# Where a weight's double words are turned into floats: two integer steps on VectorE and two passes on ScalarE, in place of three and one

## The chip, the cores and the metric

The kernel runs on one core of a Trainium2 chip. Time is device time in microseconds (us), the median of the runs shown; a profiled execution has its own time and its own span, which is the time from its first to its last instruction. The engines are named as in the profile: PE is TensorE's matmul, PEld its weight load, DVE is VectorE, ACT is ScalarE, POOL is GpSimd, SP is SyncE, which here only issues DMAs.

## The reference, cut to what matters

Three layers follow each other on a batch of 4, 576 positions, 8 heads of 64, so a model width of 512.

1. Attention. q and k are rotated by position (rope), scores are scaled by 1/8, the row maximum is subtracted, exp, division by the sum plus 1e-9, product with v.
2. First block: `xn = (x - mean) / sqrt(var + 1e-6) * g_ln`, then `x + relu(xn @ w_ch1) @ w_ch2`, with w_ch1 of 512 x 2048 and w_ch2 of 2048 x 512.
3. Second block: `h = gelu(x @ w_in)`, split in u and v; v is normalised, mixed over positions by w_sg, given b_sg, multiplied by u; `x + gated @ w_out`.

The weights w_ch1, w_ch2, w_in and w_out arrive as 64-bit floats, and the kernel sees each as two 32-bit words: a low word L and a high word H. It makes 32-bit floats of them itself. The high word has the sign, the exponent and the first 20 bits of the fraction; three more bits of fraction are the top three of the low word. So a 32-bit float is the sign of H, the rest of H (its exponent moved to the 32-bit bias) shifted left by 3, and `L >> 29` in the three places that the shift leaves free.

## The kernel before, in words

**Attention** runs in 64 units: two heads of a pair, two halves of 288 queries (HQ), four pairs, four batch entries. A unit (`unit`) computes scores of 576 keys in five chunks of 128 (`scores`, L311) into the five PSUM banks of S, takes their maximum on DVE (mx, L334), then over partitions on POOL (am, L337). Either PE adds the negative maximum to S (`add`, L392) and ACT takes exp from PSUM (L395), or DVE subtracts it (`subtract`, L376) and ACT takes exp from SBUF (L381); the second way is used once all 32 weights of the first block are stored (`stored[0] == 32`). PV (L350) multiplies by v; ACT copies the result (L357) and the row of sums (L360). There is one S and one bank for PV, so the scores of the next unit can start only when exp has read this one's.

**The first block** (`up`, `down`, L655 to L657 and L685 to L687) needs, of a batch entry, its LN (`ln`, `rest`): L477 and L479 take the reciprocals of the sums, L492 spreads them by a matmul over the PV bank, L494 multiplies, L508 and L512 subtract the mean, L524 and L528 make the two halves xh and xl of the normalised input. Weights are used as a high and a low part (`w[:, 0]`, `w[:, 1]`), since a matmul reads a shortened form of a 32-bit float (the kernel's type fp32r); so each product is three matmuls.

**Conversion.** 32 weight tiles of 128 x 512 doubles belong to the first block, 12 more (8 of w_in, 4 of w_out) to the second. `double_parts` (L37 to L56) makes a tile's floats in parts, one instruction each: the DMA of 512 KB into cd (L44), an ACT pass that scales H by 2 to the power -112, read as a float, into ce (L48), and three DVE steps: shift left by 3 (L50), join the sign from H (L52), join `L >> 29` (L55). Then the caller casts to the high part on ACT (L635, L890) and subtracts it on DVE for the low part (L637, L892). The cd words have a stride of two words in these reads. Callers are `convert` for the 32 tiles and `Weights2.split` for the 12. There are four cd and two ce buffers (two and two for the 12), and of the 32, eleven weight buffers (tags w and wx); a later tile waits with its cast until PE has used up an earlier one. The loader (L611) reads stored weights again for the later batch entries, and starts when the last of the 32 tiles has got its buffer.

**Order.** `Sched` is a planner that runs while the kernel is built: every task yields an engine, an earliest time and an assumed duration, and the planner issues next the one that can start first; a task of better rank displaces it if it could start within 0.4 (HOLD) of the displaced one's duration. Ranks: attention 0, the ends of matmul groups 1, LN 2, loads about 3, conversion 4, the matmuls of the first block 5. Each engine then runs its instructions strictly in the planned order, so the assumed durations (0.68 us for an ACT pass, 0.45 for L50, 0.7 for L52 and for L55) settle the order, and the chip settles the times. The second block, from its second part on, is written in plain program order.

Of the kernel before, what the change touches and what calls it, by code (L numbers as in the profile page):

```python
# [9 lines left out]
AF = mybir.ActivationFunctionType  # L10
ALU = mybir.AluOpType
# [17 lines left out]
I32 = mybir.dt.int32  # L29
U32 = mybir.dt.uint32  # L30


def f32(ap):
    return ap.bitcast(F32)


def double_parts(nc, q, pool, src, bufs):  # L37

    n = src.shape[1]
    d = pool.tile([128, n, 2], I32, tag="cd", name="cd", bufs=bufs[0])
    q.dma_start(out=d.rearrange("p n t -> p (n t)"), in_=src.bitcast(I32))  # L44
    yield None
    H, L = d[:, :, 1], d[:, :, 0].bitcast(U32)
    e = pool.tile([128, n], I32, tag="ce", name="ce", bufs=bufs[1])
    nc.scalar.activation(f32(e), f32(H), AF.Copy, scale=2.0 ** -112)  # L48
    yield None
    nc.vector.tensor_scalar(e, e, 3, None, ALU.logical_shift_left)  # L50
    yield None
    nc.vector.scalar_tensor_tensor(e, H, -0x80000000, e, op0=ALU.bitwise_and, op1=ALU.bitwise_or)  # L52
    yield None
    u = e.bitcast(U32)
    nc.vector.scalar_tensor_tensor(u, L, 29, u, op0=ALU.logical_shift_right, op1=ALU.bitwise_or)  # L55
    yield f32(e)  # L56


# [66 lines left out]
def latest(*xs):  # L125

    return None if any(x is None for x in xs) else max(xs)


class Attn:  # L130
# [66 lines left out]
    def split(self, x, X, at):  # L197
        nc = self.nc
        e = yield "ACT", at + 0.1, 0.43
        nc.scalar.copy(X[:, 1, :], x)  # L200
        e = yield "DVE", e + 0.1, 0.47
        nc.vector.tensor_tensor(X[:, 0, :], x, f32(X[:, 1, :]), ALU.subtract)
        return e
# [220 lines left out]
def fused_kernel(ctx, tc, q, k, v, cs, cst, w12, wi, wo, wsg, wsg4, gb, out):  # L424
    nc = tc.nc
# [169 lines left out]
    def widx(key):  # L595
        return key[2] if key[1] == 0 else 16 + 4 * key[2] + key[3]

    def wtag():
        return "wx" if len(ring) < 32 and len(ring) % (WB + WX) >= WB else "w"

    def new_w(key):

        tag = wtag()
        ring[key] = tag, wb[tag].take()
        wt[key] = (M if tag == "w" else cpool).tile([128, 2, 512], F32R, tag=tag, name=tag, bufs=WB if tag == "w" else WX)
        return wt[key]
# [7 lines left out]
    def convert(n):  # L614
        key = wq[n]
        i = widx(key)
        e = yield "SP", lambda: latest(cdb.free(), 14.0), 0.6
        slot = cdb.take()
        parts = double_parts(nc, nc.sync, cpool, w12[i], (CB, 2))
        next(parts)  # L620
        if n < 31:
            C.task(convert(n + 1), 4)
        e = yield "ACT", lambda: latest(e + L_CONV, ceb.free()), 0.68
        ce = ceb.take()
        next(parts)
        yield "DVE", e + 0.1, 0.45
        next(parts)
        yield "DVE", 0.0, 0.7
        next(parts)
        e = yield "DVE", 0.0, 0.7  # L630
        s = next(parts)
        cdb.give(slot, e)
        e = yield "ACT", lambda: latest(e + 0.1, wb[wtag()].free()) if len(ring) == n else None, 0.63
        t = new_w(key)
        nc.scalar.copy(t[:, 0, :], s)  # L635
        e = yield "DVE", e + 0.1, 0.7
        nc.vector.tensor_tensor(t[:, 1, :], s, f32(t[:, 0, :]), ALU.subtract)  # L637
        ceb.give(ce, e)
        wat[key] = e + 0.1
        yield "SP", e + 0.1, 0.6  # L640
        nc.sync.dma_start(out=f32(wsc[i]), in_=f32(t))
        stored[0] += 1
# [76 lines left out]
    def mlp_pass(g, F, halves=(0, 1), ups=None):  # L719

        n = FG[g]
        seq = [(f, hh) for f in ups or range(n) for hh in halves]
        if F in (0, 16 // n - 1):
            seq.sort(key=lambda x: x[1])
        for f, hh in seq:
            yield 0, g, F, f, hh
        for c in range(4) if ups is None else ():
            for hh in halves:
                yield 1, g, F, c, hh

    def group0():
        yield from mlp_pass(0, 0, [0])
        yield from mlp_pass(0, 1, [0], range(AHEAD))
        yield from mlp_pass(0, 0, [1])
        yield from mlp_pass(0, 1, [1], range(AHEAD))
        yield from (x for x in mlp_pass(0, 1) if x[0] or x[3] >= AHEAD)
        for F in (2, 3):
            yield from mlp_pass(0, F)
# [64 lines left out]
    C.task(select(), 3.9)  # L803
    C.task(norms(), 2, lambda: over.append("norms"))
    C.task(convert(0), 4)
    C.task(loader(), 3.5)
    pctx = ExitStack()
    parts = [*group0(), *(x for g in range(1, NG) for F in range(16 // FG[g]) for x in mlp_pass(g, F))]
# [32 lines left out]
class Weights2:  # L841
# [22 lines left out]
    def split(self, i):  # L864
        nc, t, pool, cdb, ceb, stb = self.nc, self.t, self.pool, self.cdb, self.ceb, self.stb
        src, n, k, a, z = self.items[i]
        single = src.dtype == F32
        e = yield "SP", lambda: (stb if single else cdb).free() if n + "h" in t else None, 0.6
        slot = (stb if single else cdb).take()
        if single:  # L870
            s = pool.tile([128, 576], F32, tag="st", name="st")[:, 0:z - a]
            nc.sync.dma_start(out=s, in_=src)
            if k == 0:
                nc.sync.dma_start(out=t["b"], in_=self.wsg4)
        else:
            parts = double_parts(nc, nc.sync, pool, src, (2, 2))
            next(parts)
        if i + 1 < len(self.items):
            self.C.task(self.split(i + 1), 4)
        e += 8.0  # L880
        if not single:
            e = yield "ACT", lambda: latest(e, ceb.free()), 0.68
            ce = ceb.take()
            next(parts)
            for us in (0.45, 0.7, 0.7):
                e = yield "DVE", e + 0.1 if us == 0.45 else 0.0, us
                s = next(parts)
            cdb.give(slot, e)
        e = yield "ACT", e + 0.1, 0.7
        nc.scalar.copy(t[n + "h"][:, k, a:z], s)  # L890
        e = yield "DVE", e + 0.1, 0.77
        nc.vector.tensor_tensor(t[n + "l"][:, k, a:z], s, f32(t[n + "h"][:, k, a:z]), ALU.subtract)  # L892
        if single:
            stb.give(slot, e)
        else:
            ceb.give(ce, e)
# [232 lines left out]
```

## Time and profile before

| what | value |
|---|---|
| runs, median (lowest to highest of 3) | 999.93 us (998.19 to 1001.24) |
| profiled execution, its own time | 1002.52 us |
| its span | 1000.7 us |
| mean granted TensorE clock | 0.985 |
| PE, PEld busy | 939.7 us, 867.8 us |
| DVE, ACT, POOL busy | 714.2 us, 444.6 us, 91.4 us |
| double tiles converted | 44: 13 begun from 25 to 125 us, 19 more by 320 us, 12 from 640 to 750 us |

A busy share is an average over stages: the first 125 us hold attention without the first block, from then on PE has matmuls of both, from 600 us the first block of the last batch entry with the conversion of the second block's weights, and then the second block. An engine's idle time counts only where PE is idle too, or where it makes a transfer or a buffer late.

### The profile page before, as it was taken

How to read it: one execution, taken by the hardware profiler on the slowest of the kernel's cores; microseconds unless marked ns; L12 is line 12 of the kernel's file. 1: busy time of each engine (PE TensorE's matmuls, PEld its weight loads, DVE VectorE, ACT ScalarE, POOL GpSimd, SP SyncE). 2: the span in 40 equal slices, each digit the busy share in tenths (PEclk: the TensorE clock that was granted, in tenths of full speed). 3: DMA queues.
4: the chain of work that ended last, by engine and by line, in shares of the span. 5: the costliest groups of instructions: out<-in, count | busy, mean ns of one | idle time of the engine just before them, and what ended most of it. 6: DMA issues, size and time to landing. Idle time of an engine off the chain costs nothing.

```text
span 1000.7 us, 15881 instructions
## 1 busy us (share of the span) xinstructions
PE 939.7 (94%) x6057; PEld 867.8 (87%) x6057; DVE 714.2 (71%) x1188; ACT 444.6 (44%) x901; POOL 91.4 (9%) x78
## 2 busy tenths in 40 slices
PE   4688899999998889999999999999999979999998
PEld 3566688798898778989998999999999969989998
DVE  6998666699788788865589744586553887667764
ACT  3564554665434355443235531425222546345441
POOL 1121112122000211100012110000000000000000
PEclk9899999999999899999999999999999989999999
DMA  9888444378464564653755533588763300303011
GB/s 273 240 283 263 110 106 109 104 202 258 152 207 146 189 213 134 204 163 121 251 182 145 156 128 127 192 285 273 250 204 91 90 1 12 95 2 89 1 49 48
DMA packets 93420, 153.76 MB, mean 154 GB/s; under 512 B 38048, under 2 KB 60576, under 8 KB 93344
## 3 DMA queue, kind: packets, MB, share of 16 engines
q1 hardware_dynamic: 92800, 152.16, 49.1%
q8 instruction: 48, 0.79, 0.3%
q10 hardware_dynamic: 544, 0.59, 0.2%
q14 instruction: 28, 0.23, 0.1%
HBM read 107.25 MB, written 26.21 MB: 133 GB/s over the span
## 4 chain that ended last, share of the span: by engine, by line
PE 73%; DVE 14%; DMA 5%; ACT 2%; issue 2%; POOL 2%; SPq 1%; DVEq 0%; ACTq 0%; POOLq 0%
PE PV L350 8%; PE S L311 7%; PE m L686 6%; PE m L685 6%; PE m L687 6%; PE m L655 5%; PE m L657 5%; PE m L656 5%; DVE mx L334 4%; DMA sums<-sr 3%; PE S L392 2%; PE p L1054 2%; PE p L1055 2%; PE p L1056 2%; DVE sT L376 2%
## 5 line engine op out<-in xcount | busy, mean ns | idle before, releaser
L350 PE MATMUL PV<-sT,vin 128*128 128x288 f32 x640 | 170.8, 413 | 3.6 <-ACT sr L360 1.8
L655 PE MATMUL m<-xh,w 128*128 128x288 f32 x480 | 148.0, 308 | 2.4 <-DVE h L665 2.3
L350 PEld LDWEIGHTS PV<-sT,vin 128*128 128x128 f32 x640 | 120.1, 194 | 32.7 <-ACT sr L360 2.7
L685 PE MATMUL m<-h,w 128*128 128x288 f32 x480 | 145.2, 302 | 0.0
L686 PE MATMUL m<-h,w 128*128 128x288 f32 x480 | 142.0, 296 | 0.0
L334 DVE TENSOR_REDUCE mx<-S 128x288 f32<-128x1440 f32 x64 | 106.0, 1657 | 49.9 <-PE S L311 48.8
L656 PE MATMUL m<-xl,w 128*128 128x288 f32 x480 | 141.5, 295 | 0.0
L657 PE MATMUL m<-xh,w 128*128 128x288 f32 x480 | 141.2, 294 | 0.0
L687 PE MATMUL m<-h,w 128*128 128x288 f32 x480 | 140.5, 293 | 0.0
L337 POOL PARTITION_ALL_REDUCE am<-mx x64 | 89.3, 1395 | 500.4 <-DVE mx L334 500.4
L311 PE MATMUL S<-X,K 128*128 128x288 f32 x640 | 112.6, 321 | 16.8 <-ACT X L200 10.2
L311 PEld LDWEIGHTS S<-X,K 128*128 128x128 f32 x640 | 95.5, 201 | 29.2 <-ACT sT L395 11.0
L665 DVE SCALAR_TENSOR_TENSOR h<-m,h 128x288 fp32r<-128x288 f32 x128 | 58.0, 454 | 66.6 <-ACT h L663 65.8
L655 PEld LDWEIGHTS m<-xh,w 128*128 128x128 f32 x480 | 90.0, 188 | 6.5 <-DVE h L665 3.6
L663 ACT ACTIVATE h<-m 128x288 fp32r<-128x288 f32 x128 | 52.2, 408 | 95.0 <-PE m L657 94.5
L656 PEld LDWEIGHTS m<-xl,w 128*128 128x128 f32 x480 | 90.2, 188 | 1.4
L686 PEld LDWEIGHTS m<-h,w 128*128 128x128 f32 x480 | 90.2, 188 | 1.0
L685 PEld LDWEIGHTS m<-h,w 128*128 128x128 f32 x480 | 90.0, 188 | 1.1
L657 PEld LDWEIGHTS m<-xh,w 128*128 128x128 f32 x480 | 90.3, 188 | 0.0
L687 PEld LDWEIGHTS m<-h,w 128*128 128x128 f32 x480 | 90.2, 188 | 0.0
L357 ACT COPY x<-PV 64x288 f32<-64x288 f32 x64 | 25.2, 394 | 137.8 <-PE PV L350 137.7
L395 ACT ACTIVATE sT<-S 128x576 f32<-128x576 f32 x74 | 53.6, 769 | 29.7 <-PE S L392 28.3
(149 smaller groups left out, 1848.9 us busy)
## 6 DMA issues: line engine op xcount, KB each, us to landing
w<-wsc SPq DMA_DIRECT2D x96, 512.0 KB, 4.3
X<-qin SPq DMA_DIRECT2D x124, 144.0 KB, 2.6
cd<-in_w SPq DMA_DIRECT2D x32, 512.0 KB, 6.1
wsc<-w SPq DMA_DIRECT2D x24, 512.0 KB, 3.6
qin<-in_q SPq DMA_DIRECT2D x31, 288.0 KB, 4.4
kin<-in_k SPq DMA_DIRECT2D x15, 576.0 KB, 5.0
vin<-in_v SPq DMA_DIRECT2D x40, 160.0 KB, 4.2
x1d<-x SPq DMA_DIRECT2D x32, 144.0 KB, 2.7
```

Source lines behind the costliest of these rows:

```text
L311: x = nc.tensor.matmul(S[:, ch, 0:HQ], Kb["K"][j][:, KEY0[ch]:KEY0[ch] + 128], B["X"][:, j, 1 - t, :], start=t == 0, stop=t == 1)
L334: nc.vector.tensor_reduce(mx, S[:, :, 0:HQ].rearrange("p c q -> p q c"), AX.X, ALU.max)
L337: nc.gpsimd.partition_all_reduce(am, mx, 128, bass_isa.ReduceOp.max)
L350: nc.tensor.matmul(ps, V["vin"][:, ch, 64 * j:64 * j + 128], sT[:, ch, :], start=ch == 0, stop=ch == 4)
L395: ex.append(nc.scalar.activation(sT[:, c0:c1, :], self.S[:, c0:c1, 0:HQ], AF.Exp, scale=0.125))
L655: nc.tensor.matmul(ps, w[:, 0, ms], xh[:, kc, :], start=kc == 0, stop=False)
L656: nc.tensor.matmul(ps, w[:, 0, ms], xl[:, kc, :], start=False, stop=False)
L657: nc.tensor.matmul(ps, w[:, 1, ms], xh[:, kc, :], start=False, stop=kc == 3)
L665: nc.vector.scalar_tensor_tensor(t[:, 1, :], ps, 0.0, f32(t[:, 0, :]), op0=ALU.max, op1=ALU.subtract)
L685: nc.tensor.matmul(ps, w[:, 0, ms], t[:, 0, :], start=a == 0, stop=False)
L686: nc.tensor.matmul(ps, w[:, 1, ms], t[:, 0, :], start=False, stop=False)
L687: nc.tensor.matmul(ps, w[:, 0, ms], t[:, 1, :], start=False, stop=a == n - 1)
```

## The change

The DVE step that shifts alone is gone. ACT makes `L >> 29` as a number: it reads L as an unsigned integer, multiplies by L_SCALE, a hair less than 2 to the power -29, adds L_BIAS, a hair more than -0.5, and the write to an integer rounds to the nearest. The result, 0 to 7, goes back into the place of L in cd. The first DVE step then shifts ce and joins these bits, the second joins the sign. In both callers the planner now has two ACT passes of 0.68 us behind each other and two DVE steps of 0.7, in place of one pass and 0.45, 0.7, 0.7.

```diff
+L_SCALE, L_BIAS = 2.0 ** -29 * (1 - 2.0 ** -20), 7.5 * 2.0 ** -20 - 0.5
@@ double_parts
     nc.scalar.activation(f32(e), f32(H), AF.Copy, scale=2.0 ** -112)
     yield None
-    nc.vector.tensor_scalar(e, e, 3, None, ALU.logical_shift_left)
+    nc.scalar.activation(d[:, :, 0], L, AF.Copy, scale=L_SCALE, bias=L_BIAS)
+    yield None
+    nc.vector.scalar_tensor_tensor(e, e, 3, d[:, :, 0], op0=ALU.logical_shift_left, op1=ALU.bitwise_or)
     yield None
     nc.vector.scalar_tensor_tensor(e, H, -0x80000000, e, op0=ALU.bitwise_and, op1=ALU.bitwise_or)
-    yield None
-    u = e.bitcast(U32)
-    nc.vector.scalar_tensor_tensor(u, L, 29, u, op0=ALU.logical_shift_right, op1=ALU.bitwise_or)
     yield f32(e)
@@ convert
         next(parts)
-        yield "DVE", e + 0.1, 0.45
+        e = yield "ACT", 0.0, 0.68
         next(parts)
-        yield "DVE", 0.0, 0.7
+        yield "DVE", e + 0.1, 0.7
         next(parts)
         e = yield "DVE", 0.0, 0.7
@@ Weights2.split
             next(parts)
-            for us in (0.45, 0.7, 0.7):
-                e = yield "DVE", e + 0.1 if us == 0.45 else 0.0, us
+            e = yield "ACT", 0.0, 0.68
+            next(parts)
+            for at in (e + 0.1, 0.0):
+                e = yield "DVE", at, 0.7
                 s = next(parts)
```

## Rows read from the trace of the kernel before

**Rows 1.** The page, its first part: busy time, share of the span and instructions.

```profile
PE 939.7 (94%) x6057; PEld 867.8 (87%) x6057; DVE 714.2 (71%) x1188; ACT 444.6 (44%) x901; POOL 91.4 (9%) x78
```

**Rows 2.** Windows, all engines: length, busy of each (instructions), granted clock, DMA share, GB/s.

```profile
25.00:125.00 100.00, 79.17 (x356) 61.65 (x357) 85.52 (x115) 54.96 (x102) 19.84 (x14) 0.91 0.75 224
125.00:300.00 175.00, 171.24 (x1078) 155.49 (x1077) 136.34 (x202) 94.21 (x180) 28.51 (x19) 1.00 0.55 162
300.00:340.00 40.00, 34.85 (x220) 32.09 (x219) 34.19 (x65) 18.87 (x40) 2.63 (x2) 0.91 0.38 126
640.00:750.00 110.00, 109.52 (x819) 108.23 (x818) 67.48 (x133) 37.58 (x78) 0.00 (x0) 1.00 0.78 263
```

**Rows 3.** PE's waits from 25 to 125: total us, times, longest.

```profile
PE S L392 <- POOL am L337: 14.2, 10, 3.8
```

**Rows 4.** Groups of instructions by form: busy us, mean ns, idle before.

```profile
L48 ACT ACTIVATE ce<-cd 128x512 f32<-128x512 f32 x44 | 29.1, 671 | 8.1 <-DVE w L637 5.8 <-DVE wx L637 1.6 <-DMA cd<-in_wi 0.4
L635 ACT CAST w<-ce 128x512 fp32r<-128x512 f32 x24 | 14.7, 619 | 7.2 <-DVE ce L55 7.0
L783 ACT CAST sel<-st 128x1024 fp32r<-128x1024 f32 x1 | 1.0, 1040 | 0.0
...
L52 DVE SCALAR_TENSOR_TENSOR ce<-cd,ce 128x512 int32<-128x512 int32 x44 | 31.7, 720 | 0.9
L50 DVE TENSOR_SCALAR ce<-ce 128x512 int32<-128x512 int32 x44 | 18.9, 431 | 5.1 <-ACT ce L48 4.8
```

**Rows 5.** Timeline of DVE in the first stage: start us, us, instruction.

```profile
32.06 0.42 DVE L50 TENSOR_SCALAR ce<-ce 128x512 int32<-128x512 int32 x1
32.39 1.65 DVE L334 TENSOR_REDUCE mx<-S 128x288 f32<-128x1440 f32 x1
...
91.63 0.68 DVE L52 SCALAR_TENSOR_TENSOR ce<-cd,ce 128x512 int32<-128x512 int32 x1
92.35 1.04 DVE L55 SCALAR_TENSOR_TENSOR ce<-cd,ce 128x512 uint32<-128x512 uint32 x1
93.31 0.41 DVE L50 TENSOR_SCALAR ce<-ce 128x512 int32<-128x512 int32 x1
93.65 0.44 DVE L494 TENSOR_TENSOR x<-ln,x 128x288 f32<-128x288 f32 x1
```

**Rows 6.** Timeline of ACT in the first stage.

```profile
28.95 1.21 ACT L48 ACTIVATE ce<-cd 128x512 f32<-128x512 f32 x2
...
65.75 0.66 ACT L48 ACTIVATE ce<-cd 128x512 f32<-128x512 f32 x1
66.32 1.40 ACT L395 ACTIVATE sT<-S 128x576 f32<-128x576 f32 x2
...
78.62 0.66 ACT L48 ACTIVATE ce<-cd 128x512 f32<-128x512 f32 x1
79.44 1.44 ACT L395 ACTIVATE sT<-S 128x576 f32<-128x576 f32 x2 [0.15 <-PE S L392]
```

**Rows 7.** Timeline of PE: a PV, and behind it the fourth L492 of the first LN.

```profile
97.41 2.59 PE L350 MATMUL PV<-sT,vin 128*128 128x288 f32 x10
100.89 0.41 PE L492 MATMUL ln<-rc,sel 128*128 128x288 f32 x1 [0.90 <-ACT sr L360]
```

**Rows 8.** Timelines of DVE, ACT and SP: the last tile of the 32.

```profile
328.63 0.41 DVE L50 TENSOR_SCALAR ce<-ce 128x512 int32<-128x512 int32 x1
...
336.53 0.68 DVE L55 SCALAR_TENSOR_TENSOR ce<-cd,ce 128x512 uint32<-128x512 uint32 x1
...
337.47 0.62 ACT L635 CAST wx<-ce 128x512 fp32r<-128x512 f32 x1
...
340.78 2.08 SPq L611 DMA_DIRECT2D w<-wsc  x4
```

**Rows 9.** Windows of PE alone: length, busy (instructions), clock, DMA share, GB/s.

```profile
350.00:355.00 5.00, 3.58 (x25) 1.00 1.03 412
355.00:360.00 5.00, 4.32 (x18) 1.00 1.07 345
```

## The prediction, made before the changed kernel ran

> **What bounds the kernel now.** I read the page first, then the windows by stage, then PE's waits, and only then the timelines of the places where PE waits. The page says that PE is busy 94% of the span, DVE 71%, ACT 44% [rows 1]. That is a mean; the windows show what a conversion can be worth in each stage [rows 2]. From 25 to 125 us PE is busy 79.2 of 100 us, at a granted clock of 0.91, and DVE 85.5: this stage is not PE's. From 125 to 300 PE is busy 171.2 of 175, from 640 to 750 it is busy 109.5 of 110. From 300 to 340 it loses 5.2 us, with DVE at 34.2 of 40. So only the first stage and the surroundings of 340 us have idle PE time that a faster or slower conversion could give back or add to.
>
> In the first stage PE waits 14.2 us in ten waits for the maximum over partitions, so for mx on DVE and am on POOL ahead of it [rows 3]. The order there is a chain of latency: scores, mx, am, the addition on PE, exp on ACT, the next scores. An instruction of the conversion costs time only where it stands in front of mx, of exp, or of a step of the first LN.
>
> **What the change removes and adds.** Per tile it removes L50, 0.431 us on DVE in the mean, and adds an ACT pass; the two SCALAR_TENSOR_TENSOR stay, and each still reads one strided tensor and ce, so I leave them at the 0.72 us of L52 [rows 4]. Over 44 tiles DVE loses 44 x 0.431 = 19.0 us. No row has an ACT pass that reads and writes integers at a stride of two words. From below it is bounded by the unstrided cast of as many elements, 0.62 us (L635); from above by the pass over twice as many, 1.04 us (L783), as if the strided write went at half the rate [rows 4]. I take the 0.67 of L48, which has the same strided read and the same function. Behind another pass it adds less: two L48 together take 1.21 us, so the second adds 1.21 - 0.67 = 0.54 [rows 4, 6]. ACT gains between 44 x 0.54 = 24 and 44 x 1.04 = 46 us, about 5% of its span at the most likely value.
>
> The row gives 0.67 us for the scaled copy on ACT [rows 4]. The Trainium skill's "ScalarE: Activation LUTs", section "What ACT_TABLE_LOAD costs", gives 186 ns plus 0.833 ns an element for a pass with immediate scale and bias, so an estimate of 0.61 us for 512; by it ACT would gain 44 x 0.61 = 27 us where the row gives 29.5.
>
> *First stage, 25 to 125 us.* Thirteen tiles start here. On the chain of units, L50 stood directly in front of a late mx at 32.06, which kept mx back 0.33 us (32.39 less 32.06), and directly in front of L494 of the first LN at 93.31, for 0.34 us [rows 5]. These 0.7 us go. The added pass stands behind L48; where L48 abuts an exp, it pushes it. That is so twice in this stage: at 65.75, where exp follows without a gap and would slip 0.54 us, and at 78.62, where a gap of 0.15 leaves 0.39 [rows 6]. That is 0.9 us. The other eleven passes stand in front of idle ACT time (ACT is busy 55 of 100 us here [rows 2]), which is the cover that would cost up to 0.54 us each if the planner took it away. The stage nets +0.2 us. The bounds are -0.7 (no pass in the way) and 13 x 0.54 - 0.7 = +6.3.
>
> *125 to 300 us.* PE's own work is the bound, 171.2 of 175. The 16 tiles begun here give DVE 6.9 us and take about 10 us of ACT's 81 idle ones: 0, hidden by PE. If PE's order loses that cover, at worst its 3.8 us of idle time doubles; at best they vanish.
>
> *Around 340 us.* The last of the 32 tiles has the worst rank on a DVE that is nearly full, so each of its three steps needs a turn of its own. L50 came at 328.63 and L52 right behind it, but L55 only at 336.53, after work of better rank; the cast followed at 337.47, and the loads of the weights for the next batch entry, which wait for that cast to have its buffer, at 340.78 [rows 8]. With two steps the one behind the first is the last. It starts 0.72 us after 328.63 and ends at 330.1; the cast can follow at about 330.8, some 6.7 us sooner, and the loads with it. What that is worth is bounded by the idle PE time that these loads end. They run at a DMA share of 1.03 and 1.07 from 350 to 360, and PE is busy there only 3.58 + 4.32 of 10 us [rows 9]. The idle 2.1 us are my value: PE would have the matmuls of the next batch entry to fill them. The lower end is 0: the loads stay where they are if SP has the inputs of attention (X, kin, qin) to issue first. An end below nothing is a first step that no longer fits in front of a better-ranked one and slips to the turn at 336.53; both steps then end at 338.0 (336.53 + 2 x 0.72) where L55 ended at 337.2, a loss of 0.8 us. The upper end takes the 5.2 idle us from 300 to 340 as well, 7.3 in all [rows 2, 9].
>
> *640 to 750 us.* Twelve tiles, PE idle 0.5 us of 110 [rows 2]: 0. Behind them the second block runs in program order and nothing waits for a tile.
>
> **Sum.** +0.2 + 0 - 2.1 + 0 = -1.9 us. On the profiled execution (1002.52 us, of which 1000.7 are span) that is 1000.6; the median of the runs shown is 2.6 us lower, 999.93, so the forecast is 998.0.
>
> **Rivals.** *The loads were not the hold* (time about 1000.1). The sum without the 2.1: +0.2. For it: SP issues in order, and the loads came 3.3 us after the cast, so other DMAs stood between [rows 8]. Against it: from 350 to 360 the DMA engines are over-full while PE has idle time [rows 9].
>
> *Exp waits for the added pass* (slower, about 1004.1). Thirteen passes of worst rank are planned in the first stage, each for the first moment at which ACT is free, and exp is issued by the planner together with the PE addition, not as a task that could displace them. If most of them land in front of an exp, the stage costs 6.3 us; less the 2.1 around 340, the sum is +4.2 us. It decides from some 10 of the 13 (10 x 0.54 - 0.7 - 2.1 = 2.6; 11 give 3.1), or from 7 if the gain at 340 fails too. For it: two of thirteen L48 do abut an exp. Against it: eleven don't, and the place is the same. The trace has the shift at 0.43 us on DVE and the copy at 0.67 on ACT for the same elements [rows 4]. The Trainium skill's "ScalarE: Activation LUTs", section "Rules for kernel authors", says to give additions and multiplications to VectorE, not to ScalarE; by that rule the change pays 0.24 us a tile, an estimate of 10.6 us over 44, if both engines' time weighed alike.
>
> *The first LN catches an earlier place* (faster, about 994.1). At 93.65 L494 stood behind L52, L55 and L50, 2.0 us of conversion after mx [rows 5]. Because of such delays the fourth L492 came after a whole PV that began at 97.41, and waited for its bank until 100.89 [rows 7]; ahead of that PV, with its 0.41 us, it would have run near 97.0. With some 5 us less DVE work before it (12 tiles x 0.43), the conversions may all lie ahead. The first block, which waits for this LN, then starts 3.9 us sooner (100.89 - 97.0): -3.9 - 1.9 = -5.8. For it: DVE is the fullest engine there. Against it: the planner places PE's instructions by its own times, and PV may keep its turn.
>
> That the pass doesn't do what it says is no rival for the time: it has the same length whatever it writes.
>
> **How the numbers follow.** About 3 us (0.3%) is what a measurement of this kernel can tell from no change; the limits are 996.9 and 1002.9. Forecast 0.38, loads not the hold 0.20, exp waits 0.22, LN earlier 0.20. The planner makes a new order from the first tile on, so each case scatters by some 2 us. The forecast's own range is 995.9 to 1000.1. Faster by over 0.3%: nine tenths of the LN case (0.18), and a good half of the forecast's lower side and a little of the next (0.18): 0.36. Slower: three quarters of the exp case (0.16), and 0.07 from the scatter of the others: 0.23. Within 0.3%: 0.41. The range takes in the LN case with its scatter, and the exp case short of its end: 991.5 to 1004.5.
>
> **What would show it.** In the profile after: no TENSOR_SCALAR in the conversion, 44 new passes cd<-cd near 0.67 us each, DVE near 695 us and ACT near 470; exp in the first stage seldom behind such a pass; the last cast of the 32 near 331 and the loads of stored weights before 340; windows from 350 to 360 with PE at 5 of 5 us; PE from 125 to 300 unchanged. The prediction is wrong if the new pass takes over 0.9 us, if the units of the first stage come further apart than before, if the last cast is no earlier, or if the first matmuls of the first block start more than 2 us away from where they did.

## The result, and the profile after

The changed kernel takes 991.79 us (median of 4 runs, 989.87 to 992.27); the kernel before, run beside it, 1000.46 (998.19 to 1001.24). The ratio is 0.9913, with a 95% interval of 0.9892 to 0.9935. So it is faster, by 8.7 us (6.5 to 10.8) where 1.9 were forecast. The profiled execution has a span of 989.7 us at a granted clock of 0.988. The clock is no rival: the changed kernel's four runs have 0.986 to 0.988, and no run of the kernel before with a clock in that range, of about 40 beside the experiments, took less than 998.2 us.

The page's first part, after, which answers to [rows 1]:

```profile
PE 932.6 (94%) x6052; PEld 863.6 (87%) x6052; DVE 698.5 (71%) x1145; ACT 468.0 (47%) x945; POOL 89.4 (9%) x78
```

ACT gained 23.4 us, as worked out. DVE lost 15.7, not 19.0: 1.6 of the difference are one more subtraction of the maximum (28 in place of 27). PE has five matmuls fewer, which the prediction had not foreseen: one unit less uses the addition on PE, 36 in place of 37, and its maximum is taken off on DVE. No run here shows how the write to an integer rounds, and the account of the time does not need it.

The groups of the conversion after, by form; they answer to [rows 4] (lines are higher by one or two):

```profile
L50 ACT ACTIVATE ce<-cd 128x512 f32<-128x512 f32 x44 | 29.6, 672 | 12.8 <-DMA cd<-in_wi 4.7 <-DVE w L638 4.1 <-DVE wx L638 1.9
L52 ACT ACTIVATE cd<-cd 128x512 int32<-128x512 uint32 x44 | 29.5, 670 | 0.0
...
L54 DVE SCALAR_TENSOR_TENSOR ce<-ce,cd 128x512 int32<-128x512 int32 x44 | 32.0, 728 | 2.6 <-ACT cd L52 2.3
L56 DVE SCALAR_TENSOR_TENSOR ce<-cd,ce 128x512 int32<-128x512 int32 x44 | 31.8, 722 | 0.8
```

The durations were right: 0.670 us for the new pass (0.67 had been taken), and the two joins keep their length. The Trainium skill's "ScalarE: Activation LUTs", section "What ACT_TABLE_LOAD costs", would have given an estimate of 0.61; the row decides for 0.67.

Where PE's idle time went is seen in windows of PE alone: length, PE busy (matmuls), clock, DMA share, GB/s. Before:

```profile
125.00:305.00 180.00, 176.24 (x1115) 1.00 0.55 166
305.00:400.00 95.00, 86.91 (x529) 0.96 0.53 164
400.00:640.00 240.00, 237.04 (x1583) 1.00 0.52 159
640.00:760.00 120.00, 119.52 (x889) 1.00 0.77 260
```

And after:

```profile
125.00:305.00 180.00, 178.13 (x1147) 1.00 0.57 169
305.00:400.00 95.00, 90.24 (x557) 0.96 0.61 185
400.00:640.00 240.00, 238.04 (x1600) 1.00 0.54 164
640.00:760.00 120.00, 118.45 (x862) 1.00 0.67 224
```

The difference by stage is +1.9, +3.3, +1.0 and -1.1 us of busy PE: 5.1 us of idle time gone. Five additions at 0.19 us (185 of them took 35.8 us before) are 1.0 more. The first stage seems to give 2.9 us as well (first matmul of the first block at 121.37, before at 124.26), but all of it may be chance: the kernels of experiments 4, 7 and 10, which have the same instructions as the kernel before up to 640, 315 and 342 us, have it at 122.18, 123.08 and 121.08. The granted clock from 25 to 125 us differs as well: 0.91 before, 0.93 to 0.95 in these three, 0.97 after. So a single profile places this stage to about 3 us, and stages are compared here by what several kernels have in common.

Around 340 us it came as predicted, and more. The windows that answer to [rows 9]:

```profile
350.00:355.00 5.00, 5.00 (x30) 1.00 0.00 0
355.00:360.00 5.00, 5.00 (x37) 1.00 0.02 4
```

Both are full, and the DMA engines are empty there: the loads are done. SP's timeline shows why. First before (start us, us, instruction), the rows between those of [rows 8]:

```profile
323.86 1.34 SPq L296 DMA_DIRECT2D vin<-in_v  x2
335.69 0.58 SPq L364 DMA_DIRECT2D sums<-sr  x1
...
337.00 1.19 SPq L278 DMA_DIRECT2D X<-qin  x2
```

After:

```profile
317.49 1.28 SPq L297 DMA_DIRECT2D vin<-in_v  x2
318.87 4.97 SPq L612 DMA_DIRECT2D w<-wsc  x8
328.78 0.59 SPq L365 DMA_DIRECT2D sums<-sr  x1
...
330.09 1.65 SPq L279 DMA_DIRECT2D X<-qin  x2
```

Before, SP stood still from 325.2 to 335.7, and the eight loads were behind it in its queue. What it waited for is in SP's waits from 320 to 345 (us in total, times, longest):

```profile
SPq L364 <- ACT qin L200: 10.9, 1, 10.9
```

That is the DMA of a unit's sums, which has to wait until ACT has written sr at 335.28 to 335.67 (the wait is put down to the ACT instruction next to it). The loads themselves wait for none of this. After, the planner puts all eight ahead of that DMA, into the time in which SP stood still, and ahead of the last casts, which start at 323.18.

From 640 us on, something is lost. ACT's timeline after:

```profile
663.28 0.67 ACT L50 ACTIVATE ce<-cd 128x512 f32<-128x512 f32 x1
663.85 0.67 ACT L52 ACTIVATE cd<-cd 128x512 int32<-128x512 uint32 x1
664.39 0.67 ACT L50 ACTIVATE ce<-cd 128x512 f32<-128x512 f32 x1
664.96 0.68 ACT L52 ACTIVATE cd<-cd 128x512 int32<-128x512 uint32 x1
665.96 0.41 ACT L664 ACTIVATE h<-m 128x288 fp32r<-128x288 f32 x1 [0.32 <-PE m L658]
...
666.90 0.39 ACT L557 COPY rstd<-ln 64x288 f32<-64x288 f32 x1
```

and DVE's and PE's behind it:

```profile
666.49 0.45 DVE L666 SCALAR_TENSOR_TENSOR h<-m,h 128x288 fp32r<-128x288 f32 x1
```

```profile
666.99 0.40 PE L656 MATMUL m<-xh,w 128*128 128x288 f32 x1 [1.07 <-DVE h L666]
```

The kernel has two PSUM banks for the matmuls of the first block and for its LN's sums of squares (L550). The relu (L664) is not held up by the passes: ACT waits 0.32 us for PE in front of it. What comes late is the copy L557 at 666.90, for which one of the two banks is kept although its matmuls (L550) were done at 664.13. In the kernel before, the same copy follows at once: matmuls to 677.10, copy at 677.14. So PE has only the other bank, and waits 1.07 us until both halves of the relu (L664 on ACT, L666 on DVE) have read it; the kernel before has no such wait.

### The profile page after: what moved, and what is told of

Read it like the earlier page. It is cut to its first block, busy times and chain, and to the rows that moved or that the text cites. A ratio compares the mean times of both kernels' runs of the same rounds, so it can differ in the third digit from the quotient of the medians.

```text
span 989.7 us, 15875 instructions
## 1 busy us (share of the span) xinstructions
PE 932.6 (94%) x6052; PEld 863.6 (87%) x6052; DVE 698.5 (71%) x1145; ACT 468.0 (47%) x945; POOL 89.4 (9%) x78
## 4 chain that ended last, share of the span: by engine, by line
PE 82%; DVE 9%; DMA 3%; ACT 2%; POOL 2%; issue 1%; SPq 0%; DVEq 0%; ACTq 0%
PE PV L351 11%; PE S L312 8%; PE m L687 7%; PE m L688 7%; PE m L686 7%; PE m L656 6%; PE m L658 6%; PE m L657 6%; DVE mx L335 3%; PE S L393 2%; DMA sums<-sr 2%; PE p L1057 2%; PE p L1058 2%; PE p L1059 2%; PE p L967 2%; PE p L966 2%
## 5 line engine op out<-in xcount | busy, mean ns | idle before, releaser
L338 POOL PARTITION_ALL_REDUCE am<-mx x64 | 87.3, 1364 | 489.4 <-DVE mx L335 483.3
L312 PE MATMUL S<-X,K 128*128 128x288 f32 x640 | 109.2, 315 | 17.4 <-ACT X L201 10.1
L312 PEld LDWEIGHTS S<-X,K 128*128 128x128 f32 x640 | 93.6, 197 | 27.6 <-ACT sT L396 10.9
L666 DVE SCALAR_TENSOR_TENSOR h<-m,h 128x288 fp32r<-128x288 f32 x128 | 58.2, 454 | 77.7 <-ACT h L664 76.9
L664 ACT ACTIVATE h<-m 128x288 fp32r<-128x288 f32 x128 | 52.3, 409 | 100.9 <-PE m L658 100.3
```

Of the source, the lines that this page charges most:

```text
L312: x = nc.tensor.matmul(S[:, ch, 0:HQ], Kb["K"][j][:, KEY0[ch]:KEY0[ch] + 128], B["X"][:, j, 1 - t, :], start=t == 0, stop=t == 1)
L338: nc.gpsimd.partition_all_reduce(am, mx, 128, bass_isa.ReduceOp.max)
L664: G["relu"] = nc.scalar.activation(t[:, 0, :], ps, AF.Relu).ins
L666: nc.vector.scalar_tensor_tensor(t[:, 1, :], ps, 0.0, f32(t[:, 0, :]), op0=ALU.max, op1=ALU.subtract)
```

## The experiments

Each was timed beside the kernel before. Two groups of theories were tested in turn. For the first four runs, ORDER says the gain comes from the planner's new order (it plans with two DVE steps and one more ACT pass), whatever work fills it; its rival WORK says it comes from the shorter DVE work, whatever the order.

**1. The new steps in the old order.** The new pass is issued with L48, the planner still counts 0.45, 0.7, 0.7, and its first DVE step issues nothing; PE, POOL and SP have exactly the order of before. Against the kernel before, in `double_parts`:

```diff
     nc.scalar.activation(f32(e), f32(H), AF.Copy, scale=2.0 ** -112)
+    nc.scalar.activation(d[:, :, 0], L, AF.Copy, scale=L_SCALE, bias=L_BIAS)
     yield None
-    nc.vector.tensor_scalar(e, e, 3, None, ALU.logical_shift_left)
+    yield None
+    nc.vector.scalar_tensor_tensor(e, e, 3, d[:, :, 0], op0=ALU.logical_shift_left, op1=ALU.bitwise_or)
     yield None
     nc.vector.scalar_tensor_tensor(e, H, -0x80000000, e, op0=ALU.bitwise_and, op1=ALU.bitwise_or)
-    yield None
... (the old join of L >> 29 goes)
```

> The changed instructions in the order of the kernel before: the planner is told the old steps and durations, the second ACT pass is issued in the step of the first, and the step of the shift issues nothing. PE, POOL and SP run the order of the kernel before to the instruction. Theory ORDER (the gain is made by the planner's new order, which follows from the shorter assumed DVE time): first stage +0.2 us (0.7 us of shifts gone, 0.9 us of exp behind the added pass), the last join of the 32 tiles keeps its turn and the loads of stored weights theirs, so the total is within 1.5 us of the kernel before, ratio 0.998 to 1.002. Rival WORK (19 us less on VectorE make the gain, whatever the order): most of the 8.7 us, ratio 0.991 to 0.994.

Measured 998.72 us, ratio 0.9983 (0.9972 to 0.9993): 1.7 us, at the edge of what ORDER expected.

**2. The old steps in the new order.** The planner plans as for the change, but the ACT pass issues nothing, the first DVE step issues the shift and the join of the sign together, the second `L >> 29`. Against the changed kernel:

```diff
-    nc.scalar.activation(d[:, :, 0], L, AF.Copy, scale=L_SCALE, bias=L_BIAS)
     yield None
... (the two new joins go)
+    nc.vector.tensor_scalar(e, e, 3, None, ALU.logical_shift_left)
+    nc.vector.scalar_tensor_tensor(e, H, -0x80000000, e, op0=ALU.bitwise_and, op1=ALU.bitwise_or)
+    yield None
+    u = e.bitcast(U32)
+    nc.vector.scalar_tensor_tensor(u, L, 29, u, op0=ALU.logical_shift_right, op1=ALU.bitwise_or)
```

> The old instructions in the order of the changed kernel: the planner is told two ACT passes and two DVE steps, the second ACT step issues nothing, and the first DVE step issues shift and sign join together (1.15 us where 0.7 is assumed). PE, POOL and SP run the order of the changed kernel to the instruction. ORDER: most of the gain, less what 0.43 us a tile of unplanned VectorE time costs in front of mx and of the LN steps (1 to 4 us): ratio 0.991 to 0.996. WORK: no gain, ratio 0.999 to 1.004.

Measured 997.62, ratio 0.9970 (0.9957 to 0.9983), outside what either theory expected: 1.7 and 3.0 us do not make 8.7. The windows of PE show that this kernel, too, has the gain around 340 us, and loses from 640 to 760; its first block begins at 125.36, later than in any other kernel here. That the 0.43 us a tile on DVE for which the plan has no room cause the late start is likely, but not shown.

```profile
305.00:400.00 95.00, 89.44 (x555) 0.96 0.57 180
...
640.00:760.00 120.00, 118.09 (x866) 1.00 0.75 248
```

**3 and 4. The new steps in the 32 tiles alone, and in the 12 alone,** each planned accordingly (`double_parts` takes a flag from its caller).

```diff
-def double_parts(nc, q, pool, src, bufs):
+def double_parts(nc, q, pool, src, bufs, new=True):
... (in it: the new steps if new, or else the old ones)
@@ convert (3: new = True, 4: False), Weights2.split (3: False, 4: True)
+        parts = double_parts(nc, nc.sync, cpool, w12[i], (CB, 2), new)
... (the planner's steps likewise)
```

> The change only in the 32 tiles of the first block; the 12 tiles of the second block are made the old way. The trace of the changed kernel shows PE losing 1.5 us between 660 and 670 us, where four ACT passes of two tiles (663.28 to 665.6) stand in front of the ReLU that frees a PSUM bank. If those passes are the cause, this kernel is 1.0 to 1.5 us faster than the changed one: about 990.5, ratio to before 0.990. Rival: the loss belongs to the change of batch entry there, and this kernel is as fast as the changed one, ratio 0.9913.

> The change only in the 12 tiles of the second block; PE's order is that of the kernel before to the instruction. If the four ACT passes in front of the ReLU cost 1.0 to 1.5 us, this is slower than before by as much, ratio 1.001 to 1.0015. Rival: no difference, ratio 1.000.

Measured 989.49, ratio 0.9895 (0.9880 to 0.9909), for the 32; 1002.13, ratio 1.0014 (0.9999 to 1.0029), for the 12. All of the gain is in the 32; the 12 give nothing and may cost 1.4 us, with an interval that takes in 0. Experiment 4 has the wait for h of the changed kernel, its row from PE's waits from 640 to 760:

```profile
PE m L671 <- DVE h L681: 1.1, 1, 1.1
```

and PE is busy 118.47 of those 120 us; with the old steps in the 12 (experiment 3) it is 119.52, as before. So the 1.1 us lost behind 640 belong to the new steps of the 12 tiles. It is the order that comes with them and not the passes themselves, of which the expectation of experiment 3 spoke: experiment 2, which has the new order without the passes, loses 1.4 us there, and its PE waits for the late copy itself; the row of its waits from 640 to 760:

```profile
PE m L657 <- ACT rstd L558: 1.4, 1, 1.4
```

Experiment 1, with the passes in the old order, has PE busy 119.26 us there.

Now the theories were formed anew: PLACE says that the larger part of the gain is the place of the last tile's steps and of the loads near 340 us; WORK, that every tile gives the same.

**5 and 6. The new steps in the first 13 tiles, or in the last 19.** As experiment 3, with

```diff
+        new = n < 13      # 5
+        new = n >= 13     # 6
```

> The new steps in the tiles 0 to 12 alone (those begun up to 125 us), the old ones in the other 19 of the first block and in the 12 of the second; planned accordingly. Theory PLACE (the larger part of the gain stands around 340 us and needs the last tiles' steps placed earlier; the plan here issues the loads of stored weights behind the inputs of attention as before): ratio 0.996 to 0.999, that is 1 to 3 us from the first stage and nothing at 340. Rival WORK (each tile freed of its shift gives the same): 13/32 of the 10.5 us of the version with 32 tiles, so 0.9957.

> The complement: the old steps in the tiles 0 to 12 and in the 12 of the second block, the new ones in the tiles 13 to 31. Theory PLACE: the loads stand ahead of the inputs of attention as in the changed kernel, so the jump of about 5.5 us at 340 is there, and some of the 3 us from 125 to 300: ratio 0.991 to 0.995; the matmuls of the second batch entry start near 347. Rival WORK: 19/32 of 10.5 us, so 0.9938, and no jump at 340 but an even gain.

Measured 1000.27, ratio 0.9997 (0.9981 to 1.0013), for the first 13; 992.57, ratio 0.9922 (0.9906 to 0.9937), for the last 19. The first stage gives nothing that can be measured, so the WORK theory of equal shares (0.9957) falls; the last 19 give 7.8 of the 10.5 us of experiment 3. Alone the two give 8.1 us; what is missing lies within the intervals.

**7. The place alone, without the change.** The kernel before; the last tile is ranked up from its first DVE step on.

```diff
-        yield "DVE", e + 0.1, 0.45
+        yield "DVE", e + 0.1, 0.45, 0.6 if n >= 31 else 4
```

> The kernel before with all its old steps; only the last of the 32 tiles has rank 0.6 in place of 4 from its first DVE step on, so that the planner puts its three steps behind each other and the eight loads of stored weights ahead of the inputs of attention. No engine's work changes. Theory PLACE: the jump at 340 comes without the new steps, ratio 0.993 to 0.996. Rival: the jump belongs to the shorter DVE work before it (the last tiles are ready only because DVE has less to do), ratio 0.998 to 1.001.

Measured 994.58, ratio 0.9937 (0.9921 to 0.9954): 6.3 us (4.6 to 7.9) with every engine's work on the weights as it was. What moves with the place is the store of the last tile, so that here, too, 36 units use the addition (180 matmuls of L392). SP's timeline has the loads ahead of the wait now:

```profile
325.03 4.53 SPq L611 DMA_DIRECT2D w<-wsc  x8
...
334.91 0.59 SPq L364 DMA_DIRECT2D sums<-sr  x1
```

and the windows of PE gain around 340 and not ahead of it:

```profile
125.00:305.00 180.00, 175.54 (x1110) 1.00 0.55 166
305.00:400.00 95.00, 89.02 (x563) 0.98 0.55 175
```

**8. The change without the place.** The changed kernel; the loads are planned no earlier than the kernel before plans them (342.4 on the planner's clock).

```diff
-            e = yield "SP", lambda: wb["w"].free() if len(ring) >= 32 else None, 0.6
+            e = yield "SP", lambda: latest(wb["w"].free(), 342.4) if len(ring) >= 32 else None, 0.6
```

> The changed kernel with the loads of stored weights planned no earlier than 342.4 of the planner's time, where the kernel before has them (the changed kernel has 328.8); the last casts keep their early place. Theory PLACE, in its form that the loads are what counts: 4 to 6 us of the changed kernel's gain go, ratio 0.9955 to 0.9975, first matmuls of the second batch entry near 350 again. Rival: the early cast and store count, not the loads; ratio 0.990 to 0.993 as in the changed kernel.

Measured 998.14, ratio 0.9971 (0.9959 to 0.9982): of 8.7 us, 5.8 are gone, and the two intervals are apart. The last two casts start at 324.54, about as early as in the changed kernel (323.18; before, the last one at 337.47), so it is not the cast that counts. From 345 to 400 PE is busy 52.1 us, as in the kernel before and in experiment 1, where the changed kernel and experiments 2, 3, 6 and 7, all with the loads ahead and 36 units, have 54.9 of the 55. (The first matmul of the second batch entry, the expectation's sign, says little: 347.22 here, 343.37 after and 352.82 before, but 345.89 in experiment 10, which gains nothing.) SP's timeline has the old picture, idle until the sums, and then the inputs of attention ahead of the loads:

```profile
318.86 1.55 SPq L297 DMA_DIRECT2D vin<-in_v  x2
330.10 0.58 SPq L365 DMA_DIRECT2D sums<-sr  x1
...
334.57 0.60 SPq L267 DMA_DIRECT2D qin<-in_q  x1
335.22 1.70 SPq L612 DMA_DIRECT2D w<-wsc  x3
```

The windows of PE keep the gain from 125 to 305 and lose that from 305 to 400:

```profile
125.00:305.00 180.00, 178.15 (x1142) 1.00 0.56 170
305.00:400.00 95.00, 87.42 (x516) 0.95 0.55 167
```

**9 and 10. Loads or switch.** With the loads held, the 37th unit uses the addition again (185 matmuls of L393), so experiment 8 changes two things. This pair separates them: in 9, the changed kernel, 37 units use the addition, in 10, the kernel before, 36.

```diff
-    stored = [0]
+    stored, asked = [0], [0]
+    def spare():
+        asked[0] += 1
+        return stored[0] == 32 and asked[0] > 37      # 9; in 10: return asked[0] > 36
... (unit asks spare() in place of stored[0] == 32)
```

> The changed kernel, but the 37th unit takes its maximum off by the PE addition, as in the kernel before (the changed kernel takes it off on DVE from the 37th on, one unit earlier, so has five matmuls L393 fewer). The eight loads of stored weights stay ahead of the waiting DMA of the sums. Theory LOADS (their place in SP's queue carries the 5 to 6 us at 340): ratio 0.991 to 0.9935. Rival SWITCH (the earlier switch to subtraction on DVE carries them): ratio 0.996 to 0.998, as with the loads held.

> The kernel before with one thing other: the 37th unit takes its maximum off on DVE, one unit earlier, as in the changed kernel. All steps of the conversion and the late loads stay. Theory LOADS: ratio 0.998 to 1.001. Rival SWITCH: ratio 0.993 to 0.996.

Measured 994.45, ratio 0.9941 (0.9922 to 0.9960), and 1001.44, ratio 1.0005 (0.9992 to 1.0018). The earlier switch alone gives nothing, so SWITCH by itself falls. But experiment 9 is outside what LOADS expected, too. The loads alone take the ratio from 0.9971 (experiment 8) to 0.9941, which is 3.0 us, and the switch, once the loads are early, from 0.9941 to 0.9913, which is 2.8. At each of the two steps the intervals overlap, at the first by a hair, so the sum of 5.8 us is shown and its halves are not. PE's windows agree with them: from 345 to 400 it is busy 54.2 us in experiment 9, between 52.1 and 54.9, and from 400 to 640 it is busy 236.8 to 237.7 us in the six kernels with 37 units and 237.5 to 238.1 in the six with 36, experiment 10 among the latter (238.06). There the gain is lost again ahead of 400: 85.86 busy us from 305 to 400, where the kernel before has 86.91.

**11 and 12. Both ways of converting, at an early place.** The last two tiles are ranked up (rank 0.6 from the first DVE step): 11 is otherwise the kernel before, 12 the kernel of experiment 3.

```diff
-        yield "DVE", e + 0.1, 0.45
+        yield "DVE", e + 0.1, 0.45, 0.6 if n >= 30 else 4      # 11; in 12 the same on the new first step
```

> The kernel before with its old steps; the last two of the 32 tiles have rank 0.6 from their first DVE step on, so that the last cast is planned at 320, the loads at 317.8 (7 of 8 in one go), and 35 units use the addition. By LOADS the loads are ahead of the wait as with the last tile alone, so about as much: ratio 0.992 to 0.995. Rival (each unit moved from the addition on PE to DVE gives some us of its own): 0.990 to 0.992.

> The best so far, the new steps in the 32 tiles and the old ones in the 12, and besides the last two of the 32 tiles at rank 0.6 from their first DVE step on; 35 units use the addition, loads planned at 322.8. If the new steps' gain is mostly the place of the loads, it is no better than with the old steps at the same ranks: within 0.2% of that version. Rival (the shorter DVE work gives some 3 us of its own, whatever the order): 0.3% below that version, and 0.987 to 0.9895.

Measured 994.12, ratio 0.9937 (0.9916 to 0.9957), and 990.32, ratio 0.9895 (0.9873 to 0.9917). Bringing the place still earlier than in experiment 7 adds nothing. (Both have 170 matmuls of the addition, so 34 units, not the 35 expected.) The new steps in the 32 tiles are worth about 3.8 us beside a like place; the intervals just touch. Experiments 3 and 7, both with the loads ahead and 36 units, say the same with intervals that are apart: 0.9895 (0.9880 to 0.9909) and 0.9937 (0.9921 to 0.9954), 4.2 us.

## Why the prediction came out as it did

One table holds most of it, as ratios to the kernel before; 37 and 36 are the units that use the addition:

| | loads behind the sums, 37 | behind, 36 | ahead, 37 | ahead, 36 |
|---|---|---|---|---|
| old steps | 1 | 1.0005 (0.9992 to 1.0018), experiment 10 | not run | 0.9937 (0.9921 to 0.9954), experiment 7 |
| new steps | 0.9971 (0.9959 to 0.9982), experiment 8 | not run | 0.9941 (0.9922 to 0.9960), experiment 9 | 0.9913 (0.9892 to 0.9935), the change |

The two effects add up: 6.3 us for the place with its switch and 2.9 for the steps make 9.2, and 8.7 were measured. The sign was right, and the sum was too small by 6.8 us. That the time fell inside the stated range, by 0.3 us, is luck: the forecast's own range ended at 995.9, and the lower part was there for a rival that did not happen. A time within 0.3% of the kernel before had been held likelier (0.41) than a gain beyond that (0.36).

*Durations and engine sums: right.* The new pass took 0.670 us, DVE came to 698.5 and ACT to 468.0. (The 24 us that ACT was to gain are 2.4% of its span; the 5% of the text are a share of its busy time.)

*First stage, +0.2: right within what can be measured.* Experiment 5 gives 0.9997 (0.9981 to 1.0013) for the 13 tiles that start there. The cover that could have been lost was not lost. Both terms show, small, in PE's waits from 25 to 125 us. For exp they come to 2.4 to 2.9 us in the six kernels with the old steps in the first stage in the old order (before, 4, 6, 7, 10, 11) and to 2.8 to 3.2 with the new steps there (1, 3, 5, 8, 9, 12); the profile after, with 4.7, stands alone. For the maximum they are 14.2 to 15.7 us with the old steps and 12.4 to 13.6 with the new ones in the new order. The row that answers to [rows 3]:

```profile
PE S L393 <- POOL am L338: 13.6, 10, 3.4
```

By its own sign (the first matmuls of the first block over 2 us away) the prediction would be wrong here, at 2.9 us; but the sign was set inside the scatter of 3.2 us that equal instructions have.

*125 to 300 us, 0 because PE is the bound: wrong, by 1.9 us.* The windows have 178.13 to 178.15 busy us in 180 with the new steps in the 32 tiles, planned as such (the change and experiments 3, 8, 9 and 12), and 175.54 to 176.29 with the old ones (before, 4, 7, 10 and 11). The text had given 3.8 idle us as the most that could vanish, and then took none: a stage in which PE is 98% busy can still hand back half of its idle time, if that hangs on other engines. PE's waits from 125 to 305, before:

```profile
PE S L311 <- ACT sT L395: 1.0, 2, 0.7
PE PV L350 <- ACT sr L360: 0.9, 1, 0.9
PE ln L492 <- DVE x L494: 0.5, 1, 0.5
PE S L392 <- POOL am L337: 0.5, 1, 0.5
PE ln L492 <- ACT sr L360: 0.4, 1, 0.4
```

and after:

```profile
PE PV L351 <- ACT sr L361: 0.9, 1, 0.9
PE S L393 <- POOL am L338: 0.5, 1, 0.5
PE S L312 <- ACT sT L396: 0.3, 1, 0.3
```

The LN spreads no longer wait, and exp holds the scores up for 0.3 us, not 1.0. This needs the steps and the order: with the new steps in the old order (experiment 1) PE is busy 176.22 us there, as before, and with the old steps in the new order (experiment 2) 177.01.

*Around 340 us, -2.1: right in place and sign, and the term that was mis-sized.* It measures 6.3 us by experiment 7 and 5.8 by experiment 8, between the value taken and the upper end of 7.3 that the prediction gave. Three things were wrong in it. The loads were said to wait for the last cast to have its buffer; on the chip they wait for no cast (the changed kernel issues them at 318.87, 4.3 us ahead of the last two casts), but for their turn in SP's queue, behind a DMA of sums that waits 10.9 us for ACT. It is the planner that admits the loads only after the last cast is planned, and so settles the turn. The row at 335.69 that shows this was in SP's timeline, between the ones read. The price was taken from the 10 us with the worst windows alone: PE's idle time from 305 to 400 fell by 3.3 us in the change and 2.1 in experiment 7. And the switch of the 37th unit was not in the sum at all: the earlier store lets this unit use DVE in place of five matmuls, 1.0 us of PE, and about one more us of idle time goes from 400 to 640. For experiment 7 these make 4.1; its granted clock from 305 to 400 is 0.98 in the mean of the two levels, 2.4 and 1.2 GHz, where before it is 0.96, an estimate of 0.02 x 95 = 1.9 us more. How the 5.8 us divide between the loads and the switch is what experiments 9 and 10 leave open.

*640 to 750 us, 0: wrong, by 1.1 us the other way.* That "nothing waits for a tile" holds, but the tiles' steps moved a copy of the LN that keeps a PSUM bank, and PE, busy almost all the time, waits for the other bank. The kernel with the new steps in the 32 alone avoids it.

*The rivals.* "The loads were not the hold" is refuted by experiments 7 and 8. "Exp waits for the added pass" is refuted by experiment 5. "The first LN catches an earlier place" did not happen: after, PV still stands ahead of the third and fourth spread, as PE's timeline shows beside [rows 7]:

```profile
96.20 2.59 PE L351 MATMUL PV<-sT,vin 128*128 128x288 f32 x10
99.68 0.40 PE L493 MATMUL ln<-rc,sel 128*128 128x288 f32 x1 [0.90 <-ACT sr L361]
100.63 0.40 PE L493 MATMUL ln<-rc,sel 128*128 128x288 f32 x1
```

The rule of the Trainium skill that the prediction weighed ("ScalarE: Activation LUTs", section "Rules for kernel authors": additions and multiplications to VectorE, not to ScalarE) is not borne out here: a pass of 0.67 us on ACT replaced one of 0.43 on DVE, and the kernels with it in the 32 tiles are 3.8 us (experiments 11 and 12) and 4.2 us (7 and 3) faster at a like place. Before, ACT was busy 44% and DVE 71%.

The fastest version measured is that of experiment 3: 989.49 us, 0.9895 (0.9880 to 0.9909). Its interval overlaps that of the changed kernel; what speaks for it is the wait for h that it does not have.

## What to carry to other kernels

When an order is planned by durations, a change of an instruction moves other instructions, and most of the effect may be there: run the new order with the old work, and the old order with the new work, before crediting either. For a transfer that comes late, read the whole queue in front of it; here one DMA that waited 10.9 us for its data held eight that waited for nothing. When a kernel decides by the order how a later unit works, as by `stored[0] == 32` here, count that decision as a part of the change. And a stage in which PE is 98 or 99% busy is not free of other engines: 2 us came back and 1 was lost in two such stages.

## What the runs showed of the hardware that was not expected

A strided pass on ACT from 32-bit unsigned integers to integers takes as long as one from floats to floats, 670 against 672 ns for 128 x 512. Full DMA engines need not slow PE down: from 330 to 340 us, after, PE was busy 10.00 of 10 us at a DMA share of 1.03. The idle PE time that the kernel before has from 350 to 360 at such shares [rows 9] is mostly one wait of 1.4 us of PV for exp, which it had no other matmuls to fill. And equal instructions came 3.2 us apart within the first 125 us, at granted clocks from 0.91 to 0.95.
